# A gated mix of two linear-attention blocks on one core: the issue order written by a planner inside the kernel

## The chip, the cores and the metric

The kernel runs on one core of one Trainium2 chip. The metric is the device time of one execution in microseconds (us). TensorE is PE in the profile (PEld its weight loads), VectorE is DVE, ScalarE is ACT, GpSimd is POOL, and SyncE (SP) issues the DMAs. Each engine takes its instructions in the order in which the program holds them.

## The reference, cut to what matters

```python
x = A_x                                            # (1, 2048, 576), float32
g = sigmoid((x * gate_w).sum(-1, keepdims=True))
# block A: q, k, v = x @ A_wqkv, 32 heads of 18; phi(t) = where(t > 0, t + 1, exp(t)) + 1e-6
# block B: q, k, v = x @ B_wqkv; pq, pk = q @ w_phi[h], k @ w_phi[h] for each head
#          phi = concat(softmax(p), softmax(-p))   # 36 features of a head
# both:    kv = einsum("bhsd,bhse->bhde", phi_k, v);  z = phi_k summed over s
#          o  = einsum(phi_q, kv) / (einsum(phi_q, z) + 1e-6);  a, b = o @ wo
return g * a + (1 - g) * b
```

Every output row needs kv and z summed over all 2048 rows. So there are two phases: one over all keys and values, one over all queries.

## The kernel before

x comes in 16 tiles of 128 rows (`NT` = 16). A float32 operand is split into a rounded high part and the rest (`xh`, `xl`; slots 0 to 4 and 5 to 8 of a `W` tile), and a product is the sum of three fast ones. A projection of 288 columns, half of the 576, is 14 matmuls (`proj`, L160).

**Weights.** `load_w` brings a weight in five DMAs and splits it with ACT (L118) and DVE or POOL (L120). `fold_w` multiplies B's key or query weights by w_phi on PE (L145), for five groups of heads, and ACT and DVE take the product apart (L147 to L150). Before, the start loads x of tile 0 and A's value weights, then A's key weights; B's keys are folded after tiles 0 and 1 have done their A part.

**Phase 1**, for each tile: A's values (`do_v`), A's keys with `phi_elu` (ACT exp L176, DVE L177, L178), B's keys with `softmax_exp` (DVE maxima and minima L183, L184, differences L190, L191, ACT exp L192, DVE sums L194 and reciprocal L196; POOL scales, L201), B's values. Once in two tiles `kv_pair` adds both tiles to `kv`, two PSUM banks that accumulate over all tiles (L220; 88 matmul records). B's query weights are folded in the loop at t = 3.

**Between the phases** tiles 14 and 15 (`t0`, `t1`) finish the keys and begin with the queries. A's `kv` is masked (`fold_a`, L302), summed to `z_a` (L308) and multiplied into A's output weights (`ma_units`: L327, L330; the result is the weight `MA`). B's `kv` is masked (L537), summed to `z_b` (L546) and packed into `kb_h`, `kb_l` (L558 to L562).

**Phase 2**, blocks of two tiles, woven: B's query projection and softmax (`q_b`), A's (`q_a`, `norm_a`: L350 to L357), B's normalisation (`norm_b`: POOL and DVE L363, sums L364, small steps L366 to L371, scaling L201 on DVE), transposes on PE (L417 to L433) with their evacuation by ACT (L412) and DVE (L413), the numerators (`num`, L449), and 28 matmuls for each half of an output tile (L479), a copy (L480) and a DMA.

PSUM holds two buffers each of `pq` (two banks: a whole projection), `tr` (one bank) and `bk` (one bank; `kv` has both until B's kv is folded, then `out_units`). A `tr` or `pq` buffer is free again when ACT and DVE have read it.

**What sets the order before.** The code issues its instructions to the tile framework, which schedules them itself; the order on each engine is the framework's:

```python
    with tile.TileContext(nc, schedule_with_timeline_sim=True) as tc:
        tile_gated_mix(tc, *aps, out)
```

## Time and profile before

| | us |
|---|---|
| median of 3 runs (619.95 to 620.59) | 620.36 |
| the profiled execution | 620.73 |
| its span (first to last instruction) | 618.6 |
| PE busy | 606.8 (98%) |
| DVE busy | 377.6 (61%) |
| ACT busy | 207.3 (34%) |
| POOL busy | 176.2 (28%) |
| moved by DMA | 27.93 MB |

Busy time of PE counts a matmul from its start to its modelled end, and neighbours overlap: a 288-column matmul stands with some 0.3 us and the next one starts 0.13 us later. How fast PE goes is read from the distance of starts. DVE's shares differ by phase: about a third in phase 1, over 80% in phase 2.

### The profile page before, as it was taken

How to read it: one execution, taken by the hardware profiler on the slowest of the kernel's cores; microseconds unless marked ns; L12 is line 12 of the kernel's file. 1: busy time of each engine (PE TensorE's matmuls, PEld its weight loads, DVE VectorE, ACT ScalarE, POOL GpSimd, SP SyncE). 2: the span in 40 equal slices, each digit the busy share in tenths (PEclk: the TensorE clock that was granted, in tenths of full speed). 3: DMA queues.
4: the chain of work that ended last, by engine and by line, in shares of the span. 5: the costliest groups of instructions: out<-in, count | busy, mean ns of one | idle time of the engine just before them, and what ended most of it. 6: DMA issues, size and time to landing. Idle time of an engine off the chain costs nothing.

```text
span 618.6 us, 11647 instructions
## 1 busy us (share of the span) xinstructions
PE 606.8 (98%) x5010; PEld 593.5 (96%) x5010; DVE 377.6 (61%) x628; ACT 207.3 (34%) x436; POOL 176.2 (28%) x130
## 2 busy tenths in 40 slices
PE   8999999999999999999997999999999999999997
PEld 7999999999999999999897799999999999999997
DVE  5473443334232433445789897978888888888820
ACT  6332242222122222214542434344433344333331
POOL 5013221202122222226554212433133442322300
PEclk9999999999999999999999899999999999999999
DMA  8441140000000000004411101011010110000001
GB/s 296 126 139 36 42 114 5 29 11 22 22 22 24 22 22 23 22 1 116 111 41 25 38 22 39 22 42 41 20 41 22 41 42 20 21 20 21 11 28 39
DMA packets 12659, 27.93 MB, mean 45 GB/s; under 512 B 1388, under 2 KB 1388, under 8 KB 12608
## 3 DMA queue, kind: packets, MB, share of 16 engines
q1 hardware_dynamic: 12608, 27.19, 14.3%
q8 instruction: 39, 0.64, 0.4%
q14 instruction: 12, 0.10, 0.0%
HBM read 22.47 MB, written 4.72 MB: 44 GB/s over the span
## 4 chain that ended last, share of the span: by engine, by line
PE 86%; DVE 6%; DMA 3%; ACT 2%; POOL 1%; issue 1%; SPq 0%; DVEq 0%; ACTq 0%; POOLq 0%
PE pq L160 33%; PE bk L479 19%; PE tr L160 18%; PE tr L449 4%; PE bk L220 4%; PE tr L424 2%; PE tr L327 1%; DMA wraw<-woB 1%; PE tr L417 1%; POOL W L120 1%; DMA wraw<-wAv 1%; PE pq L145 1%; DMA wraw<-wBv 1%; DVE uw L201 1%; PE tr L145 1%
## 5 line engine op out<-in xcount | busy, mean ns | idle before, releaser
L160 PE MATMUL pq<-W,xh 128*128 128x288 f32 (+1 forms) x1152 | 253.8, 300 | 0.8 <-ACT gg L344 0.8
L160 PEld LDWEIGHTS pq<-W,xh 128*128 128x128 f32 x1152 | 190.9, 189 | 2.6 <-ACT gg L344 1.1
L160 PE MATMUL pq<-W,xl 128*128 128x288 f32 (+1 forms) x640 | 186.6, 297 | 0.0
L108 POOL TENSOR_TENSOR xl<-xraw,xh 128x640 fp32r<-128x640 f32 x29 | 45.8, 1581 | 284.3 <-ACT xh L107 281.8
L160 PE MATMUL tr<-W,xh 128*128 128x288 f32 x576 | 122.6, 298 | 1.5 <-ACT ath L248 0.8
L160 PEld LDWEIGHTS pq<-W,xl 128*128 128x128 f32 x640 | 120.9, 189 | 0.5 <-issue 0.4
L160 PEld LDWEIGHTS tr<-W,xh 128*128 128x128 f32 x576 | 94.8, 189 | 3.1 <-ACT ath L248 1.0
L160 PE MATMUL tr<-W,xl 128*128 128x288 f32 x320 | 92.5, 295 | 0.0
L177 DVE TENSOR_SCALAR row<-row 128x576 f32<-128x576 f32 x32 | 25.6, 799 | 95.2 <-ACT row L176 95.2
L479 PE MATMUL bk<-W,ath 128*128 128x288 f32 x288 | 63.5, 301 | 0.4 <-ACT row L480 0.4
L194 DVE TENSOR_REDUCE ss<-uw 128x64 f32<-128x1152 f32 x32 | 43.3, 1352 | 31.8 <-ACT uw L192 31.8
L479 PE MATMUL bk<-W,vo 126*128 126x288 f32 x384 | 61.3, 299 | 0.0
L160 PEld LDWEIGHTS tr<-W,xl 128*128 128x128 f32 x320 | 60.4, 189 | 0.0
L183 DVE TENSOR_REDUCE mm<-pq 128x32 f32<-128x576 f32 x32 | 23.8, 745 | 51.5 <-PE pq L160 51.5
L479 PEld LDWEIGHTS bk<-W,vo 126*128 126x128 f32 x384 | 54.0, 189 | 0.0
L192 ACT ACTIVATE uw<-uw 128x1152 f32<-128x1152 f32 x32 | 37.3, 1167 | 36.4 <-DVE uw L191 36.4
L479 PEld LDWEIGHTS bk<-W,ath 128*128 128x128 f32 x288 | 47.2, 189 | 0.8 <-ACT row L480 0.6
L479 PE MATMUL bk<-W,atl 128*128 128x288 f32 x160 | 47.4, 297 | 0.0
L350 POOL TENSOR_TENSOR row<-row,z_a 128x576 f32<-128x576 f32 x16 | 29.0, 1813 | 54.8 <-DVE row L178 51.1
L248 ACT ACTIVATE vo<-tr 128x288 f32<-128x288 f32 x32 | 13.0, 407 | 85.2 <-PE tr L160 85.2
L201 POOL TENSOR_TENSOR uw<-uw,rs 128x1152 f32<-128x1152 f32 x16 | 34.4, 2152 | 9.5 <-DVE rs L196 9.5
L248 ACT ACTIVATE ath<-tr 128x288 f32<-128x288 f32 x32 | 12.9, 406 | 66.9 <-PE tr L160 66.9
(153 smaller groups left out, 904.1 us busy)
## 6 DMA issues: line engine op xcount, KB each, us to landing
xraw<-xT SPq DMA_DIRECT2D x30, 320.0 KB, 2.9
out<-row SPq DMA_DIRECT2D x16, 288.0 KB, 2.1
wraw<-woA SPq DMA_DIRECT2D x6, 288.0 KB
wraw<-wAq SPq DMA_DIRECT2D x5, 289.0 KB
wraw<-wBv SPq DMA_DIRECT2D x5, 288.0 KB, 4.4
wraw<-wkT SPq DMA_DIRECT2D x4, 315.0 KB
wraw<-wqT SPq DMA_DIRECT2D x4, 315.0 KB
uw<-wAk SPq DMA_DIRECT2D x4, 288.0 KB
```

The source lines that it names most:

```text
L108: eng.tensor_tensor(xl, raw, r(xh), op=ALU.subtract)
L160: PE.matmul(dst, xx[:, j, :], W[:, w, c0:c0 + n], start=(i == 0), stop=(i == len(steps) - 1))
L177: V.tensor_scalar(fx, fx, 1.0, EPS, op0=ALU.min, op1=ALU.add)
L183: V.tensor_reduce(mm[:, :32], heads(pq), op=ALU.max, axis=AX.X)
L192: A.activation(uw, uw, AF.Exp)
L194: V.tensor_reduce(ss, uw.rearrange("p s (h d) -> p (s h) d", d=DH), op=ALU.add, axis=AX.X)
L201: eng.tensor_tensor(u3, u3, rs[:, :, None].to_broadcast([P, 64, DH]), op=ALU.mult)
L220: PE.matmul(dst, vt[t % 4][:, which, 3 * gr:3 * gr + nh, :].rearrange("p h d -> p (h d)"), rhs, start=(t == 0 and first), stop=(t == NT - ...
L248: A.activation(vt[t % 4][:, which, 16 * hf:16 * hf + 16, :DH], pv[:, :HB].rearrange("p (h d) -> p h d", d=DH), AF.Copy)
L350: G.tensor_tensor(zw, f[:, :D], z_a, op=ALU.mult)
L449: PE.matmul(dst, kk[:n, i, :w], uu[:n, i, :256], start=(m == 0), stop=(m == 5))
L479: PE.matmul(po[:, :HB], l, w, start=(i == 0), stop=(i == len(steps) - 1))
```

## The change

The kernel no longer hands its instructions to the framework one by one. Pools, tiles and engines are replaced by recording objects (`Pool`, `Tile`, `View`, `Engine`). Each call becomes an `Op` with its dependencies, an engine and a cost from a formula (`Plan.weigh`). `Plan.order` gives each operation a due time: for PE, the sum of the PE costs ahead of it as the code is written; for the others, the earliest due time of what needs it or its buffer, less its own cost. `Plan.run` then walks through time with these costs: on each engine, of the operations that could start within a small slack of the earliest, it takes the one that is due first. `Plan.emit` issues the operations in that order under `tc.manual_schedule()`. Every instruction of the changed kernel therefore stands with one line, L332.

```diff
+    def order(self):
...
+        t = 0
+        for op in ops:
+            op.due = t
+            if op.eng == "PE":
+                t += op.cost
...
+        for op in reversed(ops):
+            if op.eng != "PE":
+                after = [ops[s].due for s in (*op.succ, *frees.get(op.i, ()))]
+                op.due = min(after + [op.due + 60000]) - op.cost - op.lag - self.SEM
+        return self.run(tags)
...
+        SL = {"PE": 120, "ACT": 250, "DVE": 250, "POOL": 100, "SP": 50}
...
+                first = min(s for s, _ in cand)
+                due, _, s, op = min((op.due, op.i, s, op) for s, op in cand if s <= first + SL[e])
...
+        with tc.manual_schedule():
+            for op in order:
...
-    for _ in range(5):
+    for _ in range(2):
         PE.matmul(pw[:, :HB], warm[:, :P], warm, start=True, stop=True)
...
     def kv_pair(pend):
-        for t, f, _ in pend:
-            kv_a(t, f)
-        for t, _, u in pend:
-            kv_b(t, u)
+        with plan.piece():
+            for t, f, _ in pend:
+                kv_a(t, f)
+            for t, _, u in pend:
+                kv_b(t, u)
...
-    xs = {0: load_x(0, V)}
...
+    spare = [a[:, i] for a in [wk.tile([P, 2, 640], F32, name="atl") for _ in range(2)] for i in range(2)]
+    WBk = fold_w(wkT, [None, None, None, row_tile(), row_tile()], first_x)
+    WBv = load_w(wBv, D, raws=spare + [row_tile()])
+    u0 = do_bk(xs[0])
+    u1 = do_bk(xs[1])
+    u2 = uw_tile()
+    WAv = load_w(wAv, D, raws=[None, None, None, u2[:, 0], u2[:, 1]])
+    do_v(0, xs[0], WBv, 1)
+    do_v(1, xs[1], WBv, 1)
     do_v(0, xs[0], WAv, 0)
     do_v(1, xs[1], WAv, 0)
...
     def norm_b(uw, rs, gg):
+        gb = gg[:, 1:2]
+        V.reciprocal(gb, gb)
...
-        V.tensor_scalar(den, den, gg[:, 1:2], None, op0=ALU.mult)
         V.reciprocal(den, den)
-        V.tensor_tensor(rs.rearrange("p (s h) -> p s h", s=2), rs.rearrange("p (s h) -> p s h", s=2),
-                        den[:, None, :].to_broadcast([P, 2, 32]), op=ALU.mult)
+        r2 = rs.rearrange("p (s h) -> p s h", s=2)
+        V.scalar_tensor_tensor(r2, den[:, None, :].to_broadcast([P, 2, 32]), gb, r2, op0=ALU.mult, op1=ALU.mult)
...
             A.activation(osb[:, cc], po[:, :HB], AF.Copy)
+            if t == NT - 3:
+                SP.dma_start(out[P * t:P * t + P, cc], osb[:, cc])
```

Between the phases the code is written anew: for tiles 14 and 15 all of B (keys, values, queries, `kv_b`) comes first; then A's keys and queries; B's `kv` is folded while A's projections run; `fold_a` and `ma_units` come last, woven into the first block of phase 2. The last output tile is stored in two halves. The matmuls of `kv_a` and `kv_b` stand as one unbroken piece each (`plan.piece`). What is computed stays the same.

The start, on SP's queue. `xT` is x, `wAv` and `wAk` A's value and key weights, `wkT` B's key weights as `fold_w` takes them, `phi` w_phi. Before:

```order
L103 DMA xraw_114<-xT 128x640
L117 DMA wraw_124<-wAv 128x576
L117 DMA wraw_128<-wAv 128x576
L117 DMA wraw_132<-wAv 128x576
L117 DMA uw_120<-wAv 128x576 x2
L103 DMA xraw_142<-xT 128x640
L117 DMA uw_121<-wAk 128x576 x2
```

and now:

```order
L332 DMA row_76<-phi 126x126
L332 DMA wraw_78<-wkT 126x640
L332 DMA row_76<-phi 126x504
L332 DMA wraw_81<-wkT 126x640
L332 DMA wraw_83<-wkT 126x640
L332 DMA row_85<-wkT 126x640
L332 DMA xraw_87<-xT 128x640
L332 DMA row_89<-wkT 72x640
L332 DMA xraw_91<-xT 128x640
L332 DMA atl_95<-wBv 128x576 x2
```

x of tile 0 was the first load and is now the seventh, behind w_phi and four fifths of B's key weights.

Between the phases, on DVE: the place at which PE begins with `ma_units`. `kb_l` is the last piece of B's packed kv, which frees a `tr` bank; `W_3009` and `W_3446` are the tile `MA`; `uw` is a tile's B features, `gg` its gate. Before:

```order
L183 TENSOR_REDUCE mm_3549<-pq_3513 128x32
L201 TENSOR_TENSOR uw_2818<-uw_2818,rs_2824 128x1152
L184 TENSOR_REDUCE mm_3549<-pq_3513 128x32
L562 TENSOR_TENSOR kb_l_101<-tr_3192,kb_h_100 126x252
L371 TENSOR_TENSOR rs_3117<-rs_3117,den_3364 128x64
L352 TENSOR_REDUCE den_3479<-row_3477 128x32
L364 TENSOR_REDUCE dd_3493<-row_3494 128x32
L363 TENSOR_TENSOR row_3497<-uw_3418,z_b_99 128x576
L201 TENSOR_TENSOR uw_3111<-uw_3111,rs_3117 128x1152
L562 TENSOR_TENSOR kb_l_101<-tr_3199,kb_h_100 72x2x80
L353 TENSOR_SCALAR den_3479<-den_3479,gg_3473 128x32
```

and now:

```order
L332 TENSOR_TENSOR W_3246<-bk_3384,W_3246 126x4x128
L332 RECIPROCAL gg_3362<-gg_3362 128x1
L332 TENSOR_REDUCE mm_3412<-pq_3358 128x32 x2
L332 TENSOR_SCALAR row_3422<-row_3422 128x576
L332 SCALAR_TENSOR_TENSOR row_3422<-pq_3314,row_3422 128x576
L332 TENSOR_TENSOR kb_l_3277<-tr_3410,kb_h_3273 72x2x80
L332 TENSOR_TENSOR W_3446<-tr_3438,W_3446 128x288
L332 TENSOR_REDUCE den_3457<-row_3442 128x32
L332 TENSOR_TENSOR W_3446<-tr_3444,W_3446 128x288
L332 TENSOR_SCALAR den_3457<-den_3457,gg_3043 128x32
```

The scaling of a whole tile (L201), which stood right ahead of the last piece of `kb_l`, is gone from that place, and the steps of `norm_a` for tiles 14 and 15 (`den`) now stand behind it, among the evacuations of `MA`.

## The prediction

> **What bounds the kernel now.** I read the page first, for the shares of the engines.

> ```profile
> span 618.6 us, 11647 instructions
> PE 606.8 (98%) x5010; PEld 593.5 (96%) x5010; DVE 377.6 (61%) x628; ACT 207.3 (34%) x436; POOL 176.2 (28%) x130
> ```

> PE is hardly ever idle, so a new order can only gain where PE is slower than its own work. To find those places I took the chain of waits in order of time and looked for what recurs: the kv piece of phase 1 (start, length, what) and a half of an output tile in phase 2.

> ```profile
> 126.70 3.46 PE bk L220 x85
> 160.21 3.46 PE bk L220 x85
> 193.74 3.46 PE bk L220 x85
> 260.81 3.46 PE bk L220 x85
> 511.19 3.75 PE bk L479 x28
> 548.07 3.75 PE bk L479 x28
> 607.37 7.78 PE bk L479 x56
> 615.17 0.41 ACT row L480
> ```

> In phase 1 two tiles take 193.74 - 160.21 = 33.53 us, and from 126.70 to 260.81 four such periods follow without a loss: 134.1. It is 224 matmuls and 3.46 of kv, so 0.134 us a matmul. In phase 2 two tiles take 548.07 - 511.19 = 36.88. These two periods are PE's own work. The stretches (length, then busy time of PE, PEld, DVE, ACT, POOL, clock) say where DVE comes near:

> ```profile
> 130.20:264.30 134.10, 134.10 (x1249) 133.04 (x1249) 46.98 (x64) 31.82 (x56) 30.43 (x17) 1.00 0.07 21
> 298.00:357.00 59.00, 53.85 (x378) 47.66 (x377) 51.51 (x96) 23.09 (x60) 25.41 (x17) 0.94 0.17 48
> 339.40:346.20 6.80, 5.68 (x16) 4.30 (x17) 6.71 (x15) 1.94 (x5) 2.56 (x2) 0.50 0.32 92
> 477.00:513.90 36.90, 36.90 (x286) 36.90 (x286) 30.90 (x54) 13.71 (x32) 12.73 (x8) 1.00 0.10 35
> ```

> Phase 1 uses 35% of DVE, phase 2 84%, the stretch between them 87% with PE at 91%. There PE stopped, and the timeline says why:

> ```profile
> 336.18 1.13 PE L327 MATMUL tr<-wraw,ath 128*128 128x288 f32 x4
> 340.52 2.26 PE L327 MATMUL tr<-wraw,ath 128*128 128x288 f32 x4 [3.20 <-DVE den L353]
> 336.13 0.74 DVE L364 TENSOR_REDUCE dd<-row 128x32 f32<-128x576 f32 x1
> 336.79 0.74 DVE L363 TENSOR_TENSOR row<-uw,z_b 128x576 f32<-128x576 f32 x1
> 337.46 2.68 DVE L201 TENSOR_TENSOR uw<-uw,rs 128x1152 f32<-128x1152 f32 x1
> 340.06 0.31 DVE L562 TENSOR_TENSOR kb_l<-tr,kb_h 72x160 fp32r<-72x160 f32 x1
> 337.07 1.86 POOL L108 TENSOR_TENSOR xl<-xraw,xh 128x640 fp32r<-128x640 f32 x1 [3.87 <-ACT xh L107]
> ```

> PE's next piece of MA needed a tr bank that only L562 would free, and L562 stood behind the scaling L201. The clock then fell to 0.50 for 6.8 us: the same four matmuls took 2.26 instead of 1.13. Idle 3.2, and (346.2 - 340.5)/2 = 2.8 for the clock.

> **The account of before.** For the start, one row each of the first work, of x of tile 1 on ACT and POOL, of a fold (ten records, start to start 1.12), and of the last store:

> ```profile
> 1.28 4.44 PE L66 MATMUL bk<-row 128*128 128x288 f32 x10 [1.28 <-DVE row L63]
> 5.35 0.64 PE L160 MATMUL tr<-W,xh 128*128 128x288 f32 x2
> 0.80 0.37 SPq L103 DMA_DIRECT2D xraw<-xT  x1
> 3.59 0.43 SPq L103 DMA_DIRECT2D xraw<-xT  x1
> 9.37 0.74 ACT L107 ACTIVATE xh<-xraw 128x640 fp32r<-128x640 f32 x1 [0.15 <-DMA xraw<-xT]
> 10.20 1.56 POOL L108 TENSOR_TENSOR xl<-xraw,xh 128x640 fp32r<-128x640 f32 x1 [2.58 <-DVE W L120]
> 24.30 1.28 PE L145 MATMUL tr<-row,wraw 126*128 126x126 f32 x10
> 25.42 1.28 PE L145 MATMUL pq<-row,wraw 126*128 126x126 f32 x10
> 314.14 0.59 PE L546 MATMUL tr<-atl,row 128*128 128x108 f32 x4
> 314.56 0.61 PE L546 MATMUL tr<-ath,row 128*128 128x108 f32 x4
> 615.61 0.33 SPq L483 DMA_DIRECT2D out<-row  x1
> ```

> Up to 126.70 PE did three periods less one kv piece (97.1), 56 matmuls of tile 6 (7.5) and ten folds (11.2): 115.8, so 10.9 us were lost, 5.35 of them before the first real matmul. From 260.81 to the last matmul's end at 615.15 are 354.3 us. The work in them is the rest of phase 1 (eight periods 268.2 - 104.6 - 134.1 = 29.5), eight periods of phase 2 (295.0), MA (eight groups of four at about 1.0, and 1.9 for the half-wide ones: 9.9) and 84 small matmuls of the z and kb steps (0.42 for four: 8.8), together 343.2. Lost: 11.1, of which 6.0 is the stop above. Behind the last matmul come 618.6 - 615.15 = 3.45. Loss in all: 25.5 us. Matmuls are neither added nor removed but for the three warming calls, which lie in the wait for the first load, so 25.5 is all that the change can work on.

> **The change part by part.** *The start.* Folding needs no split weights, so PE can work as soon as w_phi and the first of B's keys land; but x of tile 0 is now the seventh load. Before, the sixth load was issued at 3.59 and its data reached ACT at 9.37, with 2.1 MB ahead of it and in it. Now x of tile 0 ends 1.9 MB, so I put it at 9.0: ACT 0.74, POOL 1.56 (DVE did this for tile 0 before), and the third matmul of the first projection can start at 11.4. By then the five folds are done (5.6 of work) and two matmuls (0.3). The lost time is 11.4 - 5.9 = 5.5. After that B's softmax of tiles 0 and 1 waits on DVE behind the splits of A's values, which is free, since the next use of a pq bank is 112 value matmuls (15 us) away.

> *The second fold.* All five groups of B's queries now stand together on PE, and the softmax sums of tile 3 stand between their evacuations on DVE:

> ```profile
> L149 DVE TENSOR_TENSOR W<-tr,W 128x504 fp32r<-128x504 f32 x4 | 2.7, 683 | 3.0 <-ACT W L147 3.0
> L194 DVE TENSOR_REDUCE ss<-uw 128x64 f32<-128x1152 f32 x32 | 43.3, 1352 | 31.8 <-ACT uw L192 31.8
> L192 ACT ACTIVATE uw<-uw 128x1152 f32<-128x1152 f32 x32 | 37.3, 1167 | 36.4 <-DVE uw L191 36.4
> L201 DVE TENSOR_TENSOR uw<-uw,rs 128x1152 f32<-128x1152 f32 x16 | 23.4, 1460 | 0.3
> ```

> ACT's exp (1.17) and DVE's sum (1.35) ahead of the third group put the fourth group's tr bank at 6.9 after the first fold starts; PE is there at 6.0, and 0.3 earlier once: 1.2 lost. With 0.5 for entering the two kv pieces and folds, the stretch up to the steady period loses 5.5 + 1.2 + 0.5 = 7.2 instead of 10.9: **gain 3.7**.

> *Between the phases.* I walked along DVE's new order with start-to-start times (0.66 for 576 columns, as 336.13 to 336.79 shows; 1.28 for 1152, that is 1.36 in most rows of L201 less the same overlap), 0.2 from a matmul's end to its reader, and 0.6 for ACT's half of an evacuation.
> 1. From z_b to the first transposes of tile 14. DVE: the end of phi_elu 0.7, z_b product 0.7, two sums 1.4, small steps 0.6, scaling 1.3: 4.7. PE has 44 matmuls in that time, 5.9. No wait.
> 2. From tile 0's B queries to the transposes of tile 15. DVE: two extrema, two kb_l, eleven masks of A's kv (the rows of `fold_a`), two kb_l, a sum, two differences, small steps, scaling: 8.6. PE: 10.0. No wait.
> 3. z_a and the first of MA go one after another through one tr bank: two evacuations of 0.6 uncovered, 1.2.
> 4. Then 0.3 and 0.4 on banks of MA and on tile 14's evacuation, and 1.1 where tile 15's transposes wait for the last of MA behind a scaling.

> That is 3.0. POOL may hold DVE up as at 337.46, where the scaling took 2.68 while POOL's split ran: one such hit on the path, 2.68 - 1.46 = 1.2. So 4.2 instead of 6.0 + 5.1 of smaller losses. Of the smaller ones I keep half, 2.5, since every order has some: 6.7, **gain 4.4**. The clock does not fall in this sum, since no wait in it is near 3.2 us.

> [...]

> *The steps of norm_b* trade a small tensor_scalar for a one-column reciprocal and a tensor_tensor for a scalar_tensor_tensor of the same 64 columns: nothing, on an engine with 16% spare; without that cover some 0.1 a tile, 1.6 in all. *The end:* half of the last tile's store starts earlier; the last one is half as large: 3.45 to 3.2, **gain 0.25**.

> Sum: 620.73 - 3.7 - 4.4 - 0.25 = 612.4; the median of the runs lies 0.4 below the profiled execution: **612.0 us**.

> **The rivals.**
> *A. The stretch between the phases stays as it is* (20%). DVE has the same work there, 51.5 of 59 us, and a new order can't shorten it. Only start and end gain: 620.4 - 3.95 = 616.4. Against it: PE's stop came from one instruction's place, not from DVE's load.
> *B. A cold start* (10%). Two warming calls instead of five end near 3.1, and the first fold waits for its load until about 3.9. If the clock stays at 0.50 through the folds, they take 11.2 and end at 15.1, 3.7 after x is ready; half that if it rises midway. Time 612.0 + 2.7 = 614.7. The clock was full in the row 130.20:264.30 and only the stop of 3.2 us took it away, so gaps of 1 us speak little for it. [...]
> *C. The order fits nearly everywhere* (13%): 1.5 instead of 6.7 between the phases and 6.5 at the start: about 606.5 to 608.
> *D. Slower* (12%). A fixed order can't step aside: the exps of the last B keys stand on ACT behind three loads of woB, and the pieces of MA behind loads of woA. If both loads are late by a few us, PE idles 3 us or more twice, and each time the clock halves: 2 x 6.0 = 12 on top of 612, less 1.2 of waits that it swallows: 622.8. It decides from 8.4 us of such loss on, so one stop isn't enough. For it: the stop of before is exactly this; against it: my walk leaves 0.9 us of slack at the first place and more at the second.

> **How the numbers follow.** The forecast has 45%, A 20, B 10, C 13, D 12. What a measurement tells from no change is 0.2%, 1.2 us: faster is below 619.1, slower above 621.6. Only A's upper end can lie between, 5%; so faster 83%, same 5%, slower 12%. The range leaves out D and C's lower end: 607.0 to 618.5. The upper end is A with its 2 us of unknown waits.

> **What would show it.** Right: the kv piece behind tile 6's A keys, which stands at 126.70, starts near 119.5 (3.7 of gain, and one kv piece of 3.46 fewer is ahead of it now), periods stay 33.5 and 36.9, no idle of PE above 2 us between the phases, no second stretch at clock 0.50. Wrong: a period above 37, which would mean that DVE's order in phase 2 costs PE; the clock at 0.50 again; PE waiting at a projection's start for a pq bank.

## The result, and the profile after

The change did not make the kernel faster: 621.14 us (median of 20 runs, 619.3 to 622.43) against 620.26 for before (20 runs beside it), a ratio of 1.0016 with a 95% interval of 1.0008 to 1.0024. That is within what the prediction called no change (0.2%), where 8.4 us of gain were forecast.

The first lines of the page, and the stretches that answer to those of before (length, then busy time of PE, PEld, DVE, ACT, POOL, granted clock, DMA share, GB/s). All lines of the program are now one, the place at which the recorded operations are issued (L332 here; L331 to L335 in the experiments), so the reading goes by tile names and time.

```profile
span 620.7 us, 11672 instructions
PE 604.8 (97%) x5004; PEld 593.8 (96%) x5004; DVE 374.1 (60%) x627; ACT 203.8 (33%) x436; POOL 172.1 (28%) x131
```

```profile
80.92:84.33 3.41, 2.09 (x20) 1.99 (x18) 2.92 (x5) 2.04 (x5) 0.00 (x0) 1.00 0.55 168
84.33:87.75 3.42, 3.42 (x17) 3.42 (x16) 2.26 (x6) 0.53 (x2) 1.62 (x1) 0.50 0.63 173
...
127.09:260.88 133.79, 133.79 (x1251) 132.75 (x1249) 47.48 (x65) 30.54 (x55) 30.36 (x17) 1.00 0.07 21
298.00:357.00 59.00, 54.45 (x429) 49.66 (x428) 51.33 (x105) 19.29 (x50) 23.22 (x15) 1.00 0.11 33
360.82:364.23 3.41, 0.81 (x7) 0.81 (x8) 2.87 (x6) 0.83 (x3) 2.12 (x2) 1.00 0.33 96
364.23:367.64 3.41, 3.41 (x17) 3.40 (x17) 2.31 (x4) 1.08 (x2) 0.07 (x1) 0.50 0.00 0
```

Four periods of phase 1 take 133.8 us (134.1 before), so the steady work is as it was. Two places stand out, where the clock is at 0.50: behind the second fold (84.33) and between the phases (364.23). (The stretch that ends at 357.00 stops short of the second one.) The chain of waits has the kv piece that stood at 126.70 here:

```profile
123.70 3.46 PE bk L332 x85
```

One kv piece of 3.46 fewer is ahead of it, so 123.70 answers to 127.16 of before: 0.5 us later, where 3.7 earlier (119.5) was forecast.

**Where the time is.** To compare programs whose pieces stand in other orders, I took from all traces together the median time from one matmul's start to the next for each shape, and counted it up over each trace (591.9 us of work in every kernel, warming left out). The table gives the time that passed less that work: up to 66 us of work (the start), from 66 to 100 (the second fold), 100 to 285 (negative, since the medians lie a little above the mean there), 285 to 375 (between the phases), and to the last matmul. The zero of a column depends on these medians, so only differences between rows are read. The ratio is to before, run beside each kernel on the same chip; the losses are those of the one profiled execution, which need not be near the median (e10: 615.41 against 617.2).

| kernel | median us | ratio, 95% interval | start | 2nd fold | 100-285 | between | end |
|---|---|---|---|---|---|---|---|
| before | 620.26 | 1 | 9.3 | 1.1 | -1.3 | 12.0 | 1.8 |
| after | 621.14 | 1.0016 [1.0008, 1.0024] | 8.6 | 2.9 | -2.0 | 14.4 | 1.3 |
| e1 new code, framework's order | 618.0 | 0.9962 [0.9944, 0.998] | 11.0 | 1.1 | -1.2 | 10.4 | 1.1 |
| e2 old code, planner's order | 623.73 | 1.0049 [1.0032, 1.0066] | 8.4 | 0.2 | 0.0 | 14.1 | 2.7 |
| e6 MA ahead of features | 618.61 | 0.9972 [0.9958, 0.9987] | 8.1 | 1.4 | -2.1 | 11.8 | 1.3 |
| e12 four earlier splits off POOL | 621.35 | 1.0011 [0.9999, 1.0022] | 8.2 | 1.6 | -1.9 | 13.3 | 1.3 |
| e12b the split at the stop off POOL | 618.27 | 0.9976 [0.9964, 0.9989] | 8.8 | 1.3 | -2.2 | 11.7 | 1.3 |
| e4 DVE latency in the planner | 617.9 | 0.9951 [0.9933, 0.9969] | 8.5 | 1.7 | -1.8 | 12.1 | 0.8 |
| e3 x of tile 0 first | 623.83 | 1.0061 [1.0039, 1.0084] | 10.4 | 1.4 | -2.1 | 14.4 | 1.3 |
| e7 five warming matmuls | 620.19 | 0.9995 [0.9982, 1.0008] | 8.0 | 1.5 | -2.2 | 14.4 | 1.3 |
| e9 loads of 128 rows | 620.78 | 0.9998 [0.998, 1.0015] | 8.5 | 2.2 | -2.1 | 14.5 | 1.3 |
| e5 fold's loads in row buffers | 620.19 | 0.9991 [0.9974, 1.0007] | 8.1 | 3.8 | -1.9 | 14.4 | 1.3 |
| e5c and A's queries later | 620.24 | 0.9998 [0.9985, 1.0011] | 8.1 | 1.7 | -1.9 | 14.5 | 1.3 |
| e5d fold's loads in atl | 620.48 | 0.9991 [0.9974, 1.0008] | 8.2 | 0.7 | -1.8 | 14.4 | 1.4 |
| e8 e5d, e6 and e7 | 617.11 | 0.9947 [0.9926, 0.9969] | 8.2 | 0.7 | -1.9 | 11.9 | 1.3 |
| e1w e1 and five warming | 621.82 | 1.0013 [0.9994, 1.0032] | 10.5 | 1.1 | -1.3 | 9.2 | 1.1 |
| e14 e4 and e5d | 617.08 | 0.9940 [0.9928, 0.9952] | 8.5 | 0.7 | -1.9 | 11.7 | 0.8 |
| e10 e4, e5d and e7 | 617.2 | 0.9939 [0.9925, 0.9953] | 7.7 | 0.7 | -1.7 | 10.8 | 0.8 |
| e15 e10 and e9 | 616.0 | 0.9917 [0.9897, 0.9937] | 7.3 | 0.7 | -2.4 | 12.2 | 0.8 |

The profiled execution of after took 622.43, 1.3 more than the median. Two stretches at half clock fell into it (mean clock 0.994); most of its other runs show a mean of 0.996 or 0.997, one such stretch. The clock isn't all of the difference: two runs with one stretch took as long.

**The start.** PE's rows of after, and x of tile 0 on ACT:

```profile
1.28 2.29 PE L332 MATMUL bk<-row 128*128 128x288 f32 x4 [1.28 <-DVE row L332]
4.80 2.47 PE L332 MATMUL pq<-row,wraw 126*128 126x126 f32 x10 [1.23 <-DMA wraw<-wkT]
7.06 2.36 PE L332 MATMUL tr<-row,wraw 126*128 126x126 f32 x10
9.25 1.37 PE L332 MATMUL pq<-row,wraw 126*128 126x126 f32 x10
11.08 1.35 PE L332 MATMUL tr<-row 126*128 126x126 f32 x10 [0.46 <-DMA row<-wkT]
12.99 1.33 PE L332 MATMUL pq<-row 72*128 72x72 f32 x10 [0.56 <-DMA row<-wkT]
14.13 0.51 PE L332 MATMUL pq<-W,xh 128*128 128x288 f32 x2
```

```profile
12.01 0.74 ACT L332 ACTIVATE xh<-xraw 128x640 fp32r<-128x640 f32 x1 [0.76 <-DMA xraw<-xT]
```

The first two folds run at half clock (2.4 instead of 1.3), the last two wait for their loads, and x reaches ACT at 12.01, not 9.0. (The clock column can't show this: the trace's first record of the clock is the rise at 9.24, and what lies ahead of it is printed as 1.00.) The loads are slower than the one from which I took their speed. From the stretches of before, then of after (last column GB/s):

```profile
5.00:12.00 7.00, 6.61 (x38) 5.30 (x38) 5.33 (x9) 5.58 (x11) 4.18 (x8) 1.00 1.02 385
12.00:15.00 3.00, 3.00 (x25) 3.00 (x24) 2.71 (x5) 2.17 (x5) 0.00 (x0) 1.00 1.08 263
```

```profile
5.00:12.00 7.00, 6.54 (x38) 6.31 (x39) 2.64 (x5) 2.11 (x5) 0.00 (x0) 1.00 0.99 236
13.00:16.00 3.00, 3.00 (x23) 2.98 (x24) 1.88 (x5) 2.37 (x6) 2.89 (x2) 1.00 1.06 393
```

Before moved 385 GB/s while it loaded A's weights (128 rows of 2304 bytes) and a tile of x, and 263 at 12 to 15 us, when two pieces of B's key weights (126 rows of 2560 bytes) came, with x behind them. After loads those first: 236, and 393 once they are in.

**The second fold.** PE's row, and SP's:

```profile
82.37 1.35 PE L332 MATMUL tr<-row,wraw 126*128 126x126 f32 x10 [1.32 <-DMA wraw<-wqT]
```

```profile
42.88 34.21 SPq L332 DMA_DIRECT2D xraw<-xT  x4
78.84 1.44 SPq L332 DMA_DIRECT2D wraw<-wqT  x2
```

PE waits for a load, not for an evacuation; it was issued only at 78.84, when the fold's own first matmuls had freed a `wraw` buffer.

**Between the phases.** PE's longest stop, and what DVE and POOL did in it:

```profile
358.37 2.16 PE L332 MATMUL tr<-wraw,atl 128*64 128x288 f32 x16
363.42 0.66 PE L332 MATMUL tr<-ident,uw 128*126 128x128 f32 x4 [2.88 <-DVE W L332]
```

```profile
358.84 1.36 DVE L332 TENSOR_TENSOR uw<-uw,rs 128x1152 f32<-128x1152 f32 x1
360.11 1.80 DVE L332 TENSOR_SCALAR row<-row 128x576 f32<-128x576 f32 x1
362.04 0.76 DVE L332 SCALAR_TENSOR_TENSOR row<-pq,row 128x576 f32<-128x576 f32 x1
...
362.90 0.84 DVE L332 TENSOR_TENSOR W<-tr,W 64x288 fp32r<-64x288 f32 x2
```

```profile
359.96 1.64 POOL L332 TENSOR_TENSOR xl<-xraw,xh 128x640 fp32r<-128x640 f32 x1 [3.12 <-ACT xh L332]
```

The last two evacuations of MA (362.90), for whose `tr` banks tile 15's transposes wait, stand behind a scaling and the features of another tile, one step of which takes 1.80 instead of 0.45 beside POOL's split. This is the old stop (behind one scaling) at another place, and the clock falls behind it as before.

### The profile page after: what moved, and what is told of

It is laid out like the page before. It is cut to its first block, busy times and chain, and to the rows that moved or that the text cites. A ratio compares the mean times of both kernels' runs of the same rounds, so it can differ in the third digit from the quotient of the medians.

```text
span 620.7 us, 11672 instructions
## 1 busy us (share of the span) xinstructions
PE 604.8 (97%) x5004; PEld 593.8 (96%) x5004; DVE 374.1 (60%) x627; ACT 203.8 (33%) x436; POOL 172.1 (28%) x131
## 3 DMA queue, kind: packets, MB, share of 16 engines
q1 hardware_dynamic: 13032, 27.19, 14.1%
## 4 chain that ended last, share of the span: by engine, by line
PE 86%; DVE 9%; DMA 2%; ACT 1%; POOL 1%; issue 1%; SPq 0%; DVEq 0%; POOLq 0%
PE pq L332 35%; PE tr L332 29%; PE bk L332 22%; DVE den L332 2%; DVE uw L332 2%; DMA row<-wkT 1%; DVE row L332 1%; DVE dd L332 1%; DVE W L332 1%; POOL row L332 1%; DMA wraw<-wqT 1%; DVE atl L332 0%; DVE rs L332 0%; SPq L332 0%; DVE ss L332 0%
## 5 line engine op out<-in xcount | busy, mean ns | idle before, releaser
L332 PE MATMUL pq<-W,xh 128*128 128x288 f32 (+1 forms) x1152 | 245.7, 299 | 0.0
L332 PEld LDWEIGHTS pq<-W,xh 128*128 128x128 f32 x1152 | 189.1, 189 | 0.9 <-issue 0.2
L332 PE MATMUL pq<-W,xl 128*128 128x288 f32 (+1 forms) x640 | 186.2, 297 | 0.0
L332 PEld LDWEIGHTS pq<-W,xl 128*128 128x128 f32 x640 | 121.3, 190 | 0.0
L332 PE MATMUL tr<-W,xh 128*128 128x288 f32 x576 | 121.2, 298 | 0.0
L332 POOL TENSOR_TENSOR xl<-xraw,xh 128x640 fp32r<-128x640 f32 x30 | 48.8, 1626 | 171.8 <-ACT xh L332 156.3
L332 PEld LDWEIGHTS tr<-W,xh 128*128 128x128 f32 x576 | 95.1, 190 | 0.2
L332 PE MATMUL tr<-W,xl 128*128 128x288 f32 x320 | 93.2, 297 | 0.0
L332 PE MATMUL bk<-W,ath 128*128 128x288 f32 x288 | 66.0, 307 | 1.1 <-DVE W L332 0.6
L332 DVE TENSOR_SCALAR row<-row 128x576 f32<-128x576 f32 x32 | 16.9, 528 | 80.5 <-ACT row L332 80.5
L332 DVE TENSOR_REDUCE mm<-pq 128x32 f32<-128x576 f32 x64 | 45.5, 750 | 30.2 <-PE pq L332 30.2
L332 PEld LDWEIGHTS tr<-W,xl 128*128 128x128 f32 x320 | 60.8, 190 | 0.0
L332 DVE TENSOR_REDUCE ss<-uw 128x64 f32<-128x1152 f32 x32 | 43.1, 1348 | 28.8 <-ACT uw L332 28.6
L332 POOL TENSOR_TENSOR uw<-uw,rs 128x1152 f32<-128x1152 f32 x16 | 34.4, 2154 | 91.9 <-DVE rs L332 78.0
L332 PE MATMUL bk<-W,vo 126*128 126x288 f32 x384 | 57.1, 297 | 0.0
L332 ACT ACTIVATE ath<-tr 128x288 f32<-128x288 f32 (+2 forms) x62 | 26.3, 428 | 84.4 <-PE tr L332 77.5
L332 PEld LDWEIGHTS bk<-W,vo 126*128 126x128 f32 x384 | 53.2, 189 | 0.0
L332 ACT ACTIVATE uw<-uw 128x1152 f32<-128x1152 f32 x32 | 37.3, 1164 | 44.8 <-DVE uw L332 44.8
L332 ACT ACTIVATE vo<-tr 128x288 f32<-128x288 f32 (+2 forms) x56 | 25.5, 459 | 74.9 <-PE tr L332 66.5
L332 PEld LDWEIGHTS bk<-W,ath 128*128 128x128 f32 x288 | 47.5, 190 | 1.8 <-DVE W L332 1.0
L332 POOL TENSOR_TENSOR row<-uw,z_b 128x576 f32<-128x576 f32 x16 | 24.1, 1507 | 86.5 <-ACT uw L332 75.4
L332 PE MATMUL bk<-W,atl 128*128 128x288 f32 x160 | 47.6, 298 | 0.0
```

The source lines that it names most:

```text
L332: fn(*[a.real() if isinstance(a, View) else a for a in args], **{k: v.real() if isinstance(v, View) else v for k, v in kw.items()})
```

## The experiments

**Code or order?** After is two changes, other code and another order. e1 issues the new code by the framework's scheduler:

```diff
-        order = self.order()
-        with tc.manual_schedule():
-            for op in order:
+        if True:
+            for op in self.ops:
```

> The code of after, recorded and then handed to the framework's own scheduler in program order, without the planner's order. Theory 1 (the start is set by the loads of B's key weights, the stop between the phases by the planner's order on DVE): the start stays as in after, dense work from about 14 us and the kv piece behind tile 6's A keys at 123.6 within 1; between the phases another order, so the 3.3 us wait for the last of MA and its half clock (4.7 together) are gone unless this scheduler makes a stop of its own: 616 to 621. Rival (the rearranged code is what costs, and the planner wins some of it back): clearly above after, 623 to 627.

e2 gives the old code to the planner:

```diff
-    V, A, G, PE = nc.vector, nc.scalar, nc.gpsimd, nc.tensor
+    plan = Plan()
+    V, A, G, PE, SP = [Engine(plan, k, x) for k, x in ...]
...
+    plan.emit(tc)
```

> The code of before (A's weights and tiles 0 and 1 first, five warming matmuls), ordered by the planner. Theory 1: the start as in before, the kv piece at 126.7 within 1, since it is bound by loads and not by the order; between the phases the planner's order has stops where a DVE step runs longer than it reckons, so one stop of 2 us or more and a stretch at clock 0.50: 619 to 623. Rival (the planner's order is worth what was forecast, and the code at the start costs it): the stop behind the scaling is gone and nothing takes its place, 614 to 617.

Both ways round, the code gains and the planner costs: 0.9962 and 1.0016 with the new code (0.54% for the planner, 3.3 us), 1 and 1.0049 with the old (0.49%). The rival for e1 is refuted, and so is the one for e2, whose time lies 0.7 above the range of my theory. The loss between the phases tells the place: 10.4 in e1 against 14.4 in after. In e2 the old stop is still there: PE waits for `kb_l` (1.93 instead of 3.20), which stands behind the scaling of DVE's row at 331.48. And a second stop, with a half clock behind it, has come in at the start of phase 2 (PE's row at 388.96).

```profile
331.48 2.44 DVE L332 TENSOR_TENSOR uw<-uw,rs 128x1152 f32<-128x1152 f32 x1
```

```profile
334.20 1.78 PE L332 MATMUL tr<-wraw,ath 128*128 128x288 f32 x6 [1.93 <-DVE kb_l L332]
```

```profile
388.96 0.38 PE L332 MATMUL tr<-W,kb_h 126*126 126x256 f32 x1 [2.10 <-DVE W L332]
```

My theory for e1 was wrong on the start: it loses 11.0, not 8.6, since this scheduler issues the loads in another order.

**The place in DVE's order.** e6 adds one dependency:

```diff
+        for i in self.tail:                      # the last two evacuations of MA
+            self.elu[20].deps.add(i)             # the tensor_scalar of 360.11
+            ops[i].succ.append(self.elu[20].i)
         return self.run(tags)
```

> After with one rule more in the planner: the first step of A's query features of the tile in question (the tensor_scalar that took 1.80 us at 360.11) comes behind the last two evacuations of MA on DVE. Theory 1 (a wrong place in DVE's order makes the stop, and the stop the half clock): the wait of 2.9 to 3.3 us shrinks to about 0.8, the clock stays at 1.00 there, the time falls by 2.3 + 1.7 to 617 within 1. Rival (DVE is full there, 87% in before, and the delay only moves on): the first two output tiles of phase 2 end as late as before (387.4) and the time stays within 1 of 621.

618.61, ratio 0.9972: 2.7 us less than after (0.9972 - 1.0016 of 620). PE's rows at the old stop and at the next wait:

```profile
359.12 0.66 PE L335 MATMUL tr<-ident,uw 128*126 128x128 f32 x4 [0.70 <-DVE W L335]
...
361.45 0.35 PE L335 MATMUL tr<-W,kb_h 126*126 126x256 f32 x1 [0.69 <-DVE W L335]
```

The stop shrinks from 2.88 to 0.70 and the clock stays full in the profiled run: 14.4 - 11.8 = 2.6. Of the 2.2 + 1.7 won, 1.3 comes back, half of it in the new wait (361.45): the share that the rival had right, and why 617 within 1 was missed.

**POOL's hold on DVE.** e12 and e12b keep the order and let ACT write the low parts of x, as a copy of x, for some tiles (these low parts then hold another value):

```diff
         eng.tensor_tensor(xl, raw, r(xh), op=ALU.subtract)
+        loads.append(t)
+        if 16 < len(loads) <= 20:        # e12;  e12b: if len(loads) == 21:
+            plan.ops[-1].calls = [(nc.scalar.activation, (xl, raw, AF.Copy), {})]
```

> After, in the same order on PE, DVE and SP, but the low parts of x of the first four tiles of phase 2 are written by ACT as a copy of x, not by POOL as x less its high part (so these four tiles' low parts are wrong: only the time counts). Theory 4 (POOL's splits hold DVE up: the tensor_scalar at 360.11 took 1.80 us beside one, 0.45 without): that step takes 0.45, the stop at tile 15's transposes shrinks from 2.9 to about 1.5, and the stretch between the phases loses 2 to 3 us less: 618.5. Rival (the hits lie where DVE has time, the order is the cause): less than 0.7 gained, 620.7.

I had miscounted: e12 takes off the three splits ahead of the stop (and one before them), and leaves the one at 359.96; the tensor_scalar still took 1.79 us, and PE's stop is as long as in after:

```profile
361.98 0.66 PE L332 MATMUL tr<-ident,uw 128*126 128x128 f32 x4 [2.87 <-DVE W L332]
```

So it tests the other splits: 1.0011, nothing that can be told from after's 1.0016. e12b takes off the right one:

> After, in the same order, but the low part of x of one tile, the one whose split on POOL runs from 359.96 to 361.60, is written by ACT as a copy of x (this tile's low part is wrong: only the time counts). Theory 4 (POOL's hold is half of the stop): the tensor_scalar takes 0.45 instead of 1.80, PE's stop falls from 2.9 to about 1.5, the half clock behind it is rarer: 1.4 to 3 us less than after, 618 to 619.8. Rival (ACT's copy delays ACT's half of the last evacuations of MA, or DVE waits anyway): the stop stays above 2.3, 620.5 to 621.5.

618.27, ratio 0.9976, 2.5 us less than after. DVE's row and PE's:

```profile
358.47 0.45 DVE L332 TENSOR_SCALAR row<-row 128x576 f32<-128x576 f32 x1
```

```profile
360.43 0.66 PE L332 MATMUL tr<-ident,uw 128*126 128x128 f32 x4 [1.52 <-DVE W L332]
```

The stop falls by 1.36, as much as the step gains (1.35), and the clock stays full. So of the stop of 2.88, 1.36 is POOL's hold and 1.5 the place in the order; either one taken away gains the same 2.5 to 2.7 us, since either mostly ends the half clock: 11 of e12b's 12 runs and 10 of e6's have a mean clock of 0.999 or 1.000, one of after's 20.

**The planner's idea of DVE.**

```diff
-                o.est = max(o.est, free[e] if o.eng == e and e != "SP" else end + self.SEM)
+                o.est = max(o.est, free[e] + 120 * (e == "DVE") if o.eng == e and e != "SP" else end + self.SEM)
```

> After with one number more in the planner: a DVE step that reads the result of an earlier DVE step starts 120 ns later in its model (in the trace of after such a step starts about 35 ns after the end of the one it reads, and an independent one 84 ns before it). Nothing else is changed. Theory 1 (the planner thinks DVE faster than it is, so the order that it makes comes apart between the phases): its order puts the last evacuations of MA ahead of the features of the next tile, the wait of 2.9 us at tile 15's transposes is below 1.5 and the clock stays full there: 618 within 1. Rival (another order, other stops; what the model lacks is POOL's hold on DVE): a stop of 2 us or more remains somewhere between 300 and 380: 620 to 622.

617.9, ratio 0.9951: 4.0 us less than after by one number. PE's rows where the stop was:

```profile
357.64 0.66 PE L332 MATMUL tr<-ident,uw 128*126 128x128 f32 x4 [0.75 <-DVE W L332]
...
359.87 0.66 PE L332 MATMUL tr<-ident,row 128*128 128x128 f32 x4 [1.44 <-DVE W L332]
```

The planner now puts the evacuations of MA ahead of the other tile's features by itself, the wait is in two parts, and DVE's order in all of the stretch is another one. In the profiled run the clock still fell once there, where I had expected it full; half of its 12 runs have a mean clock of 1.000. So the gain isn't the one stop: PE's waits of over 0.15 us between 296 and 364 us add up to 5.2 us, 7.3 in after. With this number the planner is level with the framework's own order for the same code (e1: 0.9962), not ahead of it: the intervals overlap.

**The start.** Three edits, x of tile 0 first (e3), five warming matmuls (e7), and rows padded with zeros to 128 (e9):

```diff
+        plan.shift = -60000 if t == 0 else 0        # e3: added to the load's due time, in ns
         SP.dma_start(raw, xT[t].rearrange("p j n -> p (j n)"))
...
-    for _ in range(2):
+    for _ in range(5):                              # e7
...
-            SP.dma_start(raw[:n, :], src[:n, g, :])
+            m = 128 if g < 4 else 80                # e9
+            SP.dma_start(raw[:m, :], src[:m, g, :])
```

> After with the load of tile 0 of x issued first instead of seventh. Theory 2: all loads up to the last of B's key weights are needed in any case, and their sum sets the start; xh is done early, but the folds end later by the 0.33 MB that now stand ahead of them, about 1 us; the first half of the projection can begin after the third fold, so that the start gains 0.5 to 1.5: 620 within 0.7. Rival (it is the place of x alone that costs): dense work from 11.4 as forecast, a gain of 2.7: 618.

1.0061, 2.8 us more than after, where both theories had a gain. ACT has x at 3.92, and the projection begins even later, at 15.68 instead of 14.13, behind folds that wait longer for their loads:

```profile
6.11 2.47 PE L334 MATMUL pq<-row,wraw 126*128 126x126 f32 x10 [2.54 <-DMA wraw<-wkT]
9.80 2.47 PE L334 MATMUL tr<-row,wraw 126*128 126x126 f32 x10 [1.22 <-DMA wraw<-wkT]
15.68 0.51 PE L334 MATMUL pq<-W,xh 128*128 128x288 f32 x2
```

So x was not what the first projection waited for; the folds were, and what stands ahead of their loads delays them. That disposes of the step of the prediction that priced the start by x.

> After with five warming matmuls as in before instead of two. Theory 2 (the folds wait for their loads, whether the clock is full or not): the clock is full from about 5 instead of 9.2, the first folds take 1.3 instead of 2.4, and the time they win goes into waits for the next load; 621 within 0.6. Rival (the cold start, rival B of the prediction): 2.7 less, 618.4.

0.9995, 1.3 us less than after, with an interval that touches after's. The folds run warm (1.28 to 1.58 each, where the first two of after took 2.47 and 2.36), and then wait for the last load:

```profile
12.40 1.33 PE L332 MATMUL pq<-row 72*128 72x72 f32 x10 [0.62 <-DMA row<-wkT]
13.54 0.51 PE L332 MATMUL pq<-W,xh 128*128 128x288 f32 x2
```

Rival B of the prediction (2.7) is right in kind; 0.6 of the profiled start is left of it, the rest goes into the wait for loads.

> After with the key and query weights of B and w_phi padded with zero rows in memory, so that a load has 128 rows (80 for the last piece) instead of 126 (72); everything else stands in the same order. Theory 2 (a load of 126 rows isn't spread evenly, some of the 16 DMA engines get more of it, and so the start's loads come late): xh of tile 0 on ACT at about 10 instead of 12.0, dense work 1.5 to 2.5 us earlier, the wait of 1.3 us in the second fold shorter: 617 to 619. Rival (rows of 2560 bytes are slow in themselves, or the chip's memory gives no more at that time): the same times of landing, 621 within 0.7.

```profile
5.00:11.80 6.80, 6.80 (x36) 6.80 (x37) 1.95 (x4) 1.94 (x5) 0.00 (x0) 1.00 1.02 304
```

304 GB/s instead of 236: the loads are faster, but the time can't be told from after's (0.9998, 1.1 us less, the intervals overlap); the clock came up only at 10.8 in this run and the folds were the bound. So loads of 128 rows came faster here than those of 126, and why isn't shown. The rival's long rows are not enough: x has rows of 2560 bytes too, and a tile of it was among the loads at 385 GB/s in before. What keeps 304 from 393 stays open.

**The second fold.** Three ways to load the last two pieces of B's query weights earlier:

```diff
-            WBq = fold_w(wqT)
+            WBq = fold_w(wqT, [None, None, None, row_tile(), row_tile()])     # e5, e5c
+        plan.shift = 104000 * (src.shape[1] == 578)    # e5c: A's queries not before 104 us of the plan
+            late = wk.tile([P, 2, 640], F32, name="atl")                      # e5d
+            WBq = fold_w(wqT, [None, None, None, late[:, 0], late[:, 1]])
```

> After with the last two pieces of B's query weights loaded into two buffers of another pool, so that their loads don't wait for the fold's first matmuls to free a buffer. Theory 1 (that wait is the loss of the second fold): the wait of 1.3 us for the load at 82.4 goes and the half clock of 3.4 us behind it too (1.7): 618 within 0.7, the stretch from the fold to the next tile 3 us shorter. Rival (DVE's and ACT's evacuations of the folds are late as well, as was forecast): a wait of 1.2 for a tr or pq bank takes its place and the half clock stays: 620.5 to 621.

The wait grew. SP's rows, and PE's:

```profile
76.75 0.80 SPq L332 DMA_DIRECT2D row<-wqT  x2
78.41 2.56 SPq L332 DMA_DIRECT2D wraw<-wAq  x3
```

```profile
82.77 1.35 PE L332 MATMUL tr<-row 126*128 126x126 f32 x10 [2.16 <-DMA row<-wqT]
```

The loads are issued 2.1 us earlier, but six loads are then under way together, up to 83 us.

> The kernel with the last two pieces of B's query weights in buffers of another pool, and with the loads of A's query weights moved behind the next tile of x, so that they don't share the DMA engines with B's. Theory 2 (in the run without that move the loads came early enough, but all six went on together, until 82.4): the last pieces land near 80, the wait of 1.3 to 2.3 us and the half clock behind it are gone, 1.5 to 2 us less than after: 619.3 within 0.6. Rival (the fold is then late by its evacuations on ACT and DVE): a wait of about 1 us for a tr or pq bank, 620.5.

With A's query loads out of the way PE still waits 1.30, which neither the theory nor the rival had: the loads stand on SP's queue behind the fourth tile of x, which waits until 76.6 for its buffer, and are issued right behind it, at 76.68.

> After with the last two pieces of B's query weights in a buffer that is free from about 17 us, so that their loads stand ahead of all the x tiles on SP's queue (in the two runs before they still stood behind the fourth, which waits until 76.7 for its buffer). Theory 3 (the loss of the second fold is the place of two loads on SP's queue): no wait of PE on a load at the fold, no half clock behind it, and the stretch from 77 to 92 us loses 1.1 as in before instead of 2.8: 619.3 within 0.6. Rival (evacuations late by the exp and the sum of tile 3, the 1.2 of the prediction): a wait of 1 us on a tr bank, 620.5.

Loaded at 17 us, they cost nothing at the fold:

```profile
81.03 1.38 PE L332 MATMUL tr<-row,atl 126*128 126x126 f32 x10 [0.17 <-DVE W L332]
```

The second fold loses 0.7 instead of 2.9, and the rival (an evacuation late by 1.0) is refuted. The time is 0.9991, 1.5 less than after, with intervals that touch. Of the 2.2, 1.7 was a half clock that, by the mean clocks (0.994 in 2 of 20), few runs of after have beside the one between the phases.

**Together.** e8 joins e5d, e6 and e7; e14 joins e4 and e5d; e10 is e14 with five warming matmuls; e15 is e10 with the rows of e9.

> After with three edits together: five warming matmuls, the last two pieces of B's query weights loaded early, and the features of the next tile behind the last evacuations of MA on DVE. Theory (the losses add: 2.7 between the phases, 1.5 at the second fold, 0.5 to 1 at the start): 616.3 within 1, the fastest of all. Rival (DVE passes the delays on): 618, no better than the edit of MA alone.

> The same with two warming matmuls. Theory (the gains add): 617.9 less 1 for the second fold, 616.9, and 0.5 to 1 above the one with five. Rival (nothing to gain at the second fold, once no half clock follows it): 617.9.

> The planner with 120 ns between dependent DVE steps, the last two pieces of B's query weights loaded early, and five warming matmuls. Theory (the gains add): 617.9 of the first edit, less 1 for the second fold, less 0.5 to 1 for the start: 616.2, faster than every kernel before. Rival (with five warming matmuls the clock's steps fall badly, as in the kernel that lost 3 us by them): 619 to 621.

> The fastest kernel so far (DVE latency in the planner, early loads of the last query weights, five warming matmuls) with key and query weights and w_phi padded to 128 rows. Theory (the even loads gave their time to folds at half clock): the last of B's key weights lands 1 us earlier, the first projection starts at 12.2 instead of 13.17, 616.2. Rival (the memory gives no more at the start, whatever the rows): 617.2 as without.

e8: 0.9947, e14: 0.9940, e10: 0.9939. All three are faster than before by 0.5 to 0.6%; the five warming matmuls (e10 against e14) make no difference in the medians, against my 0.5 to 1. e15 adds the loads of 128 rows and has the lowest time: 616.0 us, 0.9917 [0.9897, 0.9937]. There the first projection begins at 12.69, and between 5 and 12 us 306 GB/s are moved instead of e10's 276. That these loads pay where the folds run warm fits this, but the intervals of e15 and e10 overlap, and the clock came up at 4.1 in e15's trace and at 6.0 in e10's, so it isn't shown.

**A loss that lies in the phase of the clock.**

> The code of after with the framework's own scheduler and five warming matmuls. Theory (the clock comes up earlier and the folds that wait for no load run faster): 0.5 to 1.3 less than with two, 617. Rival (all of the start is loads): 618 as with two.

> The code of after with the framework's scheduler and five warming matmuls once more, for its trace: 11 of its 12 runs took about 4 us more than the profiled one, at a mean clock of 0.989 to 0.994 instead of 1.000. Theory (steps of half clock, each 3.4 us long and 1.7 us lost, in the stretch between the phases and at the folds): a run near 622 with two to four of them, each behind a wait that was also there in the first trace. Rival (late loads at the start): 622 with a clock of 1.000 and a start 4 us later.

e1w was 1.0013 against e1's 0.9962, 3.2 us more, although its first profiled execution took 617.89. A second profile of it caught an execution of 621.57, whose stretches are these:

```profile
9.39:12.80 3.41, 1.38 (x10) 1.19 (x10) 1.95 (x4) 1.43 (x5) 1.55 (x1) 1.00 1.06 260
12.80:16.21 3.41, 2.27 (x11) 2.30 (x12) 1.73 (x3) 2.07 (x4) 1.54 (x1) 0.50 1.07 357
16.21:19.63 3.42, 3.42 (x17) 3.42 (x17) 2.10 (x5) 2.73 (x7) 0.73 (x1) 0.50 0.99 374
19.63:23.04 3.41, 3.41 (x16) 3.41 (x16) 3.31 (x6) 2.66 (x5) 1.60 (x2) 0.50 0.14 53
```

The folds wait for loads with the clock just up, it falls at 12.80 and stays at half for three stretches of 3.41 us: 5.1 us lost, 4 of them against the first profile. There PE waited 1.8 and 1.1 us, in two stretches of the clock, and no half clock followed; here 2.0 us of waiting fell into the one stretch of the first line. The theory holds, though the place is the start and not also the stretch between the phases. In e1, with two warming matmuls, the clock of the profiled run came up only at 13.4, behind its waits for loads, and so had nothing to lose in them.

## Why the prediction was wrong, point by point

Two steps of the sum failed: the price of the start, and the walk along DVE between the phases, with a half clock behind its last wait put at nothing. What the runs showed in their place:

- **Bound and steady work** were right: periods of 33.45 (133.79 / 4) in phase 1, 36.8 in phase 2, and some 25 us of loss as all there is to win.
- **"x of tile 0 ... I put it at 9.0"**: it came at 12.01. The step took the bytes at the speed of another load. (The load of 3.59 that it calls the sixth is the seventh; its 2.1 MB are right.) The fact that counts stood in the trace of before and was not looked up: only 263 GB/s while two pieces of these very weights came. And x was not the gate (e3): the folds were, and the first projection began at 14.13, where I had its third matmul at 11.4. I let them run warm, 5.6 us; from 4.80 to 14.13 they took 9.3, with half clock and waits for loads.
- **"1.2 lost" at the second fold**: 2.9, and by other things, a load behind a buffer (1.3) and a half clock (1.7). Where the loads were early (e5d), PE waited 0.17 for the tr bank that I had computed, and 0.33 behind the fold. Two DMAs of the step that moved were left out of the walk.
- Start and second fold up to 285 us of work lose 9.5 instead of 9.1: **gain 3.7 was -0.4**.
- **Between the phases**, gain 4.4 was a loss of 2.4 (14.4 against 12.0), 6.8 us off. Item 3, the two waits on z_a (1.2), was right: 1.3. Items 1 and 2 (no wait) were 0.6 and 0.4. Where item 4 had 0.3 and 0.4, PE waited 0.98, 0.46 and 0.63. Its last wait, 1.1, and the hit of 1.2 by POOL make 2.3 of the stop of 2.88, and behind the stop came 1.7 of half clock, which the sum had at nothing. That is 4.8 of the 6.8; the rest is about the half of the smaller losses (2.5) that was struck off without a reason. What made the waits longer is that DVE's steps take longer than I walked them. The small steps of norm_b, which I took at 0.6 in all:

```profile
309.02 0.66 DVE L332 TENSOR_TENSOR dd<-dd,rs 128x64 f32<-128x64 f32 x1
309.71 0.19 DVE L332 SCALAR_TENSOR_TENSOR den<-dd 128x32 f32<-128x32 f32 x1
309.94 0.35 DVE L332 RECIPROCAL den<-den 128x32 f32<-128x32 f32 x1
310.33 0.28 DVE L332 SCALAR_TENSOR_TENSOR rs<-den,gg,rs 128x64 f32<-128x64 f32 x1
310.65 1.36 DVE L332 TENSOR_TENSOR uw<-uw,rs 128x1152 f32<-128x1152 f32 x1
```

  They take 1.63: each starts 0.03 to 0.04 after the end of the one it reads, while independent steps overlap by 0.08 (the sum of 311.92 ends at 312.66, the next step starts at 312.58), and the first takes 0.66 beside POOL's products, which end at 309.59, where one with POOL idle takes 0.21 (322.09). The planner made the same mistake with dependent steps as I did, and e4 shows what it was worth to the order: 4 us. How much of each wait comes from it isn't shown apart.
- **"one such hit on the path" (1.2)** was the right number for the stop (1.36 in e12b), at a step of which I had not thought: a tensor_scalar with one input, 1.80 beside POOL's split and 0.45 without it. I had reckoned with a hit on the scaling alone, a product of two inputs. Other hits (e12) cost nothing that could be measured: 1.0011 against after's 1.0016.
- **"The clock does not fall, since no wait is near 3.2"**: it fell behind 2.88, and behind 1.32 at the fold. The length of a wait alone isn't what decides (last section).
- **The end**: 3.45 to 3.3 (620.7 - 617.4), 0.15 of the 0.25; the last blocks lose 0.5 less.
- **The rivals.** The time lies where none stood, between A's upper end (618.5) and D (622.8), so the 5% for no change had no case behind it. D is nearer, and half right: a fixed order that can't step aside, and a half clock behind the stop. But it priced two stops behind loads between the phases, where there was one behind DVE; the rest of the miss is the start's. A had the stretch between the phases unchanged, where it lost 2.4 more, and kept the gain of the start, which did not come. Its reason, that a new order can't shorten DVE's work there, is neither shown nor refuted: e6, e12b and e4 bring the stretch back to 11.7 to 12.1, hardly below before's 12.0, but the framework's order on the new code goes below it (10.4 in e1). B was there, hidden under late loads.

## What to carry to other kernels

Before pricing a start by bytes, look up the rate in the very stretch of the trace where the same tensor is loaded, and count the loads of a moved step as well as its matmuls. A planner is only as good as its model of the engine that is nearly full: compare its times with a trace step by step, dependent steps above all, before its order is believed. Where a stop can take the clock with it, one that is cut by half can gain more than its length (e12b: 1.36 us of stop, 2.5 us of time).

## What the hardware showed that I had not expected

I counted PE's busy time in each window of this grid, from the first rise of the clock to the last matmuls. In before and after, three windows at full clock were followed by half clock: 0.81 us busy (after, 360.82), 1.37 (before, 335.95) and 2.09 (after, 80.92). The lowest that were not have 2.43 (after, 336.92) and 2.57 (before, 329.12). In the experiments 1.38 was followed by it twice (e1w, 9.39; e2, 386.92), but 1.52 in e2 (332.31) was not, nor was 2.31 in e6 (80.41). Since 2.09 was and 1.52 was not, busy time alone doesn't settle it. The price is 1.7 us for each window at 0.50, and 5.1 in e1w, where three in a row stay half (12.80 to 23.04). It differs from one execution to the next of the same program: the 20 runs of after have mean clocks of 0.994 to 0.999.
